# One operation for the home expert's number, own routing for the last list but one, and a new order of work, in a fused attention and mixture-of-experts kernel

## The chip, the cores and the metric

The kernel runs on one core of a Trainium2 chip. The metric is the device time of one execution in microseconds (us), as the median of several runs. Shorter is better.

## The reference

Four batches of 12288 query rows (128 channels) attend to a pooled key map, and each result row is then sent through one of eight experts. What matters of it:

```python
kv_pool = kv.reshape(B, H // r, r, W // r, r, C).mean(axis=(2, 4))
k = v = kv_pool.reshape(B, -1, C) @ w_sr          # 768 keys a batch
s = scale * (q @ k.transpose(0, 2, 1))
a = softmax(s)
x = (a @ v).reshape(-1, C)                        # 49152 rows
logits = x @ w_gate                               # 8 experts
e = argmax(logits, axis=1)
out = softmax(logits)[e] * (relu(x @ w1[e]) @ w2[e])
```

## The kernel before, in words

The rows are worked on in 96 tiles of 512, 24 to a batch. For each tile the attention comes first: four groups of 128 queries, each with its scores on TensorE (PE), the maximum on VectorE (DVE, `maxima`), the exponentials on ScalarE (ACT, `exps`) and a block transpose on DVE (`turn_p`). The turned probabilities go out to memory (`send_p`, in two halves) and come back in another layout (`fetch_p`, two halves), on SP's DMA queue. ACT rounds them to their high half (`high_p`, three pieces), GpSimd (POOL) makes the low half (`low_p`), and PE multiplies both with the values (`values`). Nearly every product is made of three matmuls like this, out of high and low halves (`mm3`, lines 424 to 427), so each operand has a `high` and a `low` step; `high` and `low` themselves are lines 409 and 412. Tiles 0 and 1 go another way: their probabilities are turned on PE (`turn_first`, line 709).

Then comes the routing, by units of one or two tiles (tiles 0 and 1 of a batch are units of their own, the rest are pairs; 52 units). It makes the logits, the one-hot choice of expert and the gate. Each batch has one home expert, the one that the most rows of its first tile choose. `home` (line 904) counts votes on PE and makes, on DVE, `av`, its maximum `top`, the mask `pick` (line 917), the product `pks` of the mask with the expert numbers (line 920), and its sum, the number of the home expert (line 924). That number is read by SP, which loads this expert's weights. All rows of a batch go through the home expert (`experts`: eight blocks of `first`, `high_h`, `low_h` and `second`, then the output). Rows that chose another expert, the strays, are written into lists in memory: `ranks` and `lists` make their places on PE and DVE, `places` on POOL, `order_x` on DVE, and `put` (line 974) scatters one small row for each token, four indirect DMAs for a tile, on POOL. A few stray lists are then read back and done at the end (`ending`), and their rows are scattered over the output (line 1326).

A unit's lists are written when the next unit is routed, so the last unit but one is written with the routing of tile 95, and the last unit behind it, its scatters at a late due time (`put_last`).

The order of work on every engine and queue is written out by hand. Each step has a due time in units of which a tile has 16: a base time from the table `AT` (and from the tile's number), to which the table `MOVE` adds a correction for one named step. A heap (`Plan.run`) takes the steps by due time and issues their instructions, and every engine then runs its own in that order:

```python
key = (*of, fn.__name__, *(x for x in args if not isinstance(x, (float, dict))))
plan.at(t + MOVE.get(key, 0.0), fn, *args)
```

Until tile 0's experts begin the scores have two pairs of PSUM banks; after it they have one, and three banks serve the experts' hidden blocks (lines 391, 1385 to 1394).

Of the kernel before, what the change touches and what calls it, by code (L numbers as in the profile page):

```python
# [21 lines left out]
P = 128  # L22
# [22 lines left out]
    'lists_after': 6.0, 'put_after': 1.5, 'put_last': 66.0, 'turn_y': 2.13, 'move_y': 0.65, 'fetch_y': 6.15,  # L45
# [34 lines left out]
    ('all', 'ask'): 0.0608, ('all', 'fill_pads'): -4.1416, ('all', 'go', 2): -0.6912, ('all', 'go', 3): -5.5634,  # L80
    ('keys', 0, 'pool_head', 4, 0, 4): -0.398, ('keys', 0, 'pool_head', 4, 2, 1): 0.0428, ('keys', 1, 'low_kv', 0):
    0.5914, ('keys', 1, 'pool', 0, 2): -3.677, ('keys', 1, 'pool', 5, 3): 0.1037, ('keys', 1, 'rows', 0, 1): 9.8605,
    ('moe', 0, 'first', 1): -1.0383, ('moe', 0, 'first', 3): -0.706, ('moe', 0, 'first', 5): -1.1562, ('moe', 0,
    'first', 7): -0.6168, ('moe', 0, 'low_h', 6): 0.9976, ('moe', 0, 'second', 0): -0.8796, ('moe', 0, 'second', 2):
    -0.9594, ('moe', 1, 'low_h', 1): 0.785, ('moe', 1, 'low_h', 3): 0.7933, ('moe', 1, 'low_h', 7): 0.7654, ('moe',
    16, 'fetch_y'): 0.2111, ('moe', 2, 'low_h', 2): 0.8672, ('moe', 2, 'low_h', 4): 0.8488, ('moe', 21, 'high_h',
    6): 1.0052, ('moe', 21, 'high_h', 7): 1.7775, ('moe', 21, 'second', 4): 0.5351, ('moe', 22, 'high_h', 0): 0.369,
    ('moe', 22, 'high_h', 1): 0.423, ('moe', 22, 'low_h', 7): -0.241, ('moe', 22, 'second', 1): 1.006, ('moe', 23,
    'low_h', 1): -0.607, ('moe', 3, 'low_h', 1): 0.8385, ('moe', 3, 'low_h', 3): 1.2639, ('moe', 3, 'low_h', 5):
    1.0453, ('moe', 3, 'low_h', 7): 1.1582, ('moe', 4, 'low_h', 0): 0.9424, ('moe', 40, 'order_y'): -0.5162, ('moe',  # L90
    41, 'low_h', 4): 0.0097, ('moe', 44, 'fetch_y'): 0.3182, ('moe', 44, 'move_y'): -0.0224, ('moe', 44, 'order_y'):
    -0.1192, ('moe', 45, 'first', 0): 0.1827, ('moe', 45, 'first', 1): -0.5133, ('moe', 45, 'first', 6): -0.6373,
    ('moe', 45, 'high_h', 0): 0.5733, ('moe', 45, 'high_h', 1): 0.2381, ('moe', 45, 'high_h', 2): -0.1508, ('moe',
    45, 'high_h', 4): 0.3703, ('moe', 45, 'high_h', 5): 0.3419, ('moe', 45, 'second', 0): 0.0096, ('moe', 45,
    'second', 1): -0.6265, ('moe', 45, 'second', 4): 0.9203, ('moe', 46, 'fetch_y'): -5.214, ('moe', 46, 'high_h',
    1): 0.4473, ('moe', 46, 'low_h', 2): 0.1479, ('moe', 46, 'order_y'): 0.2087, ('moe', 46, 'store_y'): 0.9537,
    ('moe', 47, 'fetch_y'): -0.0101, ('moe', 47, 'first', 5): -0.82, ('moe', 47, 'high_h', 3): 1.2641, ('moe', 47,
    'high_h', 6): 1.1188, ('moe', 47, 'low_h', 3): 0.0473, ('moe', 47, 'low_h', 6): 0.7816, ('moe', 47, 'low_h', 7):
    0.1061, ('moe', 47, 'second', 0): -0.0776, ('moe', 47, 'second', 1): 0.0425, ('moe', 47, 'second', 4): 0.0501,
    ('moe', 47, 'second', 6): 0.0208, ('moe', 48, 'first', 5): -0.5455, ('moe', 48, 'first', 6): -2.5799, ('moe',  # L100
    48, 'first', 7): -6.5649, ('moe', 48, 'high_h', 1): 0.1424, ('moe', 48, 'low_h', 2): -0.0333, ('moe', 48,
    'low_h', 4): -0.4459, ('moe', 48, 'second', 0): -0.1822, ('moe', 48, 'second', 3): -1.6033, ('moe', 64,
    'fetch_y'): 0.274, ('moe', 64, 'move_y'): 0.6093, ('moe', 68, 'low_h', 7): -0.076, ('moe', 68, 'order_y'):
    -5.5601, ('moe', 69, 'copy_y'): -0.3826, ('moe', 69, 'fetch_y'): -2.4744, ('moe', 69, 'high_h', 4): 0.0321,
    ('moe', 69, 'high_h', 5): 0.0878, ('moe', 69, 'high_h', 6): -0.0689, ('moe', 69, 'high_h', 7): 0.0837, ('moe',
    69, 'low_h', 2): -0.0943, ('moe', 69, 'low_h', 6): -0.2325, ('moe', 69, 'second', 2): 0.6919, ('moe', 69,
    'second', 4): 0.0109, ('moe', 69, 'store_y'): -0.4167, ('moe', 70, 'fetch_y'): -0.0171, ('moe', 70, 'first', 0):
    -1.5594, ('moe', 70, 'first', 1): -0.0868, ('moe', 70, 'first', 5): -0.1211, ('moe', 70, 'high_h', 1): 1.4475,
    ('moe', 70, 'high_h', 4): 0.8979, ('moe', 70, 'high_h', 5): -0.3782, ('moe', 70, 'low_h', 1): -0.0695, ('moe',
    70, 'low_h', 3): 2.9785, ('moe', 70, 'low_h', 5): -0.0731, ('moe', 70, 'move_y'): -0.1231, ('moe', 71, 'first',  # L110
    0): -0.1207, ('moe', 71, 'first', 1): 0.0174, ('moe', 71, 'first', 4): -0.1249, ('moe', 71, 'first', 5): 0.3023,
    ('moe', 71, 'first', 6): -0.4535, ('moe', 71, 'high_h', 4): 0.0746, ('moe', 71, 'high_h', 5): 0.0835, ('moe',
    71, 'high_h', 6): -0.0512, ('moe', 71, 'low_h', 0): -0.0323, ('moe', 71, 'low_h', 1): 0.5487, ('moe', 71,
    'low_h', 2): -0.0736, ('moe', 71, 'low_h', 4): 0.5119, ('moe', 71, 'second', 2): 0.1089, ('moe', 71, 'second',
    6): -0.5769, ('moe', 72, 'first', 0): 0.2274, ('moe', 72, 'first', 5): -0.5999, ('moe', 72, 'high_h', 0):
    0.0123, ('moe', 72, 'high_h', 7): 0.1144, ('moe', 72, 'second', 0): 0.3824, ('moe', 90, 'low_h', 3): 0.6174,
    ('moe', 91, 'high_h', 7): 0.5069, ('moe', 91, 'second', 7): 0.1429, ('moe', 92, 'first', 0): -0.7256, ('moe',
    92, 'high_h', 0): 0.039, ('moe', 92, 'high_h', 1): 0.262, ('moe', 92, 'high_h', 7): 1.5258, ('moe', 92,
    'order_y'): -2.2243, ('moe', 92, 'store_y'): 3.9584, ('moe', 93, 'copy_y'): -0.2268, ('moe', 93, 'fetch_y'):
    -1.0243, ('moe', 93, 'first', 5): -0.7666, ('moe', 93, 'high_h', 5): 0.2107, ('moe', 93, 'low_h', 1): 0.1114,  # L120
    ('moe', 93, 'low_h', 5): -0.2504, ('moe', 93, 'order_y'): -0.0152, ('moe', 93, 'second', 7): -1.7719, ('moe',
    94, 'low_h', 1): 1.2426, ('moe', 94, 'low_h', 6): 1.0005, ('moe', 95, 'second', 1): -0.8013, ('moe', 95,
    'second', 2): -0.8019, ('route', 0, 'gate', 2): 3.3863, ('route', 0, 'go', 0): 1.5515, ('route', 0, 'norm'):
    2.1006, ('route', 1, 'gate', 0): 0.1309, ('route', 1, 'go', 21): -0.2161, ('route', 1, 'go', 22): -0.5587,
    ('route', 1, 'go', 23): 2.8345, ('route', 1, 'keep_x'): 9.1447, ('route', 1, 'onehot'): -0.1545, ('route', 1,
# [100 lines left out]
def tile_pooled_attention_top1_moe(ctx: ExitStack, tc, q, kv, w_sr, w_gate, w1, w2, out):  # L226
# [578 lines left out]
    def route(t, i, own):  # L805
# [98 lines left out]
        def home():  # L904
# [18 lines left out]
            with nc.allow_low_precision("small whole numbers are exact"):  # L923
                nc.vector.reduce_sum(out=num, in_=pks, axis=AX.X)
# [517 lines left out]
```

## Time and profile before

| | |
|---|---|
| median of 3 runs | 1992.07 us (1991.38 to 1992.39) |
| the profiled execution | 1995.03 us |
| its span, first to last instruction | 1993.3 us |
| mean granted clock of TensorE | 0.995 |
| PE, DVE, ACT, POOL busy | 98%, 83%, 70%, 74% of the span |
| DMA queue of SP (q1) | 77.2% of 16 engines |

How to read it: PE is busy nearly all the time, so its idle time is the place to look. The rows below come from views of that one execution. In a row of a timeline the number in square brackets is the time that the engine stood idle before the instruction, and behind it what ended the wait. In a table of stretches each engine has its busy time in the stretch and, in brackets, its number of instructions; then come the granted clock of TensorE as a share of 2.4 GHz, the share of the 16 DMA engines, and what they moved.

### The profile page before, as it was taken

The page shows a single profiled execution, that of the slowest core. Times are in us where ns is not written, and L with a number is a line of the kernel's source. Part 1 is how long each engine was busy: PE and PEld are TensorE (multiplying, and loading weights), DVE is VectorE, ACT ScalarE, POOL GpSimd, SP SyncE. Part 2 cuts the span into 40 slices and gives each one's busy share as a digit, 9 for nine tenths or more (in the row PEclk, how much of TensorE's full clock was granted, in tenths as well). Part 3 has the DMA queues.
Part 4 walks back from the last instruction along what each step waited for, and adds up shares of the span by engine and source line. Part 5 has one row for each costly group of instructions (what it writes and reads, how often), then busy time and mean ns, then how long its engine had stood idle before and what let it go on. Part 6 is the DMA issues. An engine that isn't in the chain of part 4 may idle for free. (4 is left out here: it accounts for less than half of the span.)

```text
span 1993.3 us, 31428 instructions
## 1 busy us (share of the span) xinstructions
PE 1953.7 (98%) x9482; PEld 1643.1 (82%) x9482; DVE 1645.6 (83%) x3066; ACT 1386.3 (70%) x2718; POOL 1484.0 (74%) x1567
## 2 busy tenths in 40 slices
PE   7899999999999999999999999999999999999997
PEld 6788888888788888888878888888887888888885
DVE  5888888988878888888888889888878788888764
ACT  4677676777676767676767767777777676767663
POOL 0567777777786787778787678777778677778884
PEclk9999999999999999999999999999999999999998
DMA  5899999998687788887678878788777777777662
GB/s 160 213 255 256 241 253 238 246 236 236 205 254 244 231 260 237 249 246 243 209 234 244 255 235 243 232 255 256 228 210 241 228 227 221 229 217 234 213 206 62
DMA packets 504085, 457.57 MB, mean 230 GB/s; under 512 B 240208, under 2 KB 443985, under 8 KB 503520
## 3 DMA queue, kind: packets, MB, share of 16 engines
q1 hardware_dynamic: 491296, 455.06, 77.2%
q0 software_dynamic: 12608, 0.40, 0.5%
q8 instruction: 77, 1.26, 0.3%
q14 instruction: 104, 0.85, 0.1%
HBM read 230.76 MB, written 225.25 MB: 229 GB/s over the span
## 5 line engine op out<-in xcount | busy, mean ns | idle before, releaser
L412 POOL TENSOR_TENSOR pt<-pt,pth 128x1024 fp32r<-128x1024 f32 x282 | 675.8, 2412 | 201.8 <-ACT pth L409 176.6
L1221 ACT ACTIVATE hh<-ps 128x512 fp32r<-128x512 f32 x772 | 464.7, 602 | 502.4 <-PE ps L427 487.9
L1227 DVE SCALAR_TENSOR_TENSOR hlow<-ps,hh 128x512 fp32r<-128x512 f32 x768 | 517.9, 682 | 66.7 <-ACT hh L1221 65.9
L644 DVE TENSOR_REDUCE nmax<-ps 128x1 f32<-128x768 f32 x384 | 366.0, 953 | 147.2 <-PE ps L427 143.1
L976 POOL DMA_INDIRECT xs<-row,dst x384 | 381.1, 993 | 135.4 <-issue 85.8
L667 DVE STREAM_TRANSPOSE pb<-prob 128x768 f32<-128x768 f32 x376 | 364.5, 969 | 42.7 <-ACT prob L652 39.5
L652 ACT ACTIVATE prob<-ps,nmax 128x768 f32<-128x768 f32 x384 | 345.0, 898 | 45.1 <-DVE nmax L644 40.6
L426 PE MATMUL ps<-hlow,wt 128*128 128x512 f32 x768 | 302.8, 394 | 6.9 <-DVE hlow L1227 6.9
L425 PE MATMUL ps<-hh,wt 128*128 128x512 f32 x768 | 304.8, 397 | 0.0
L427 PE MATMUL ps<-xh,wt 128*128 128x512 f32 x768 | 302.6, 394 | 1.6 <-POOL wt L412 1.6
L427 PE MATMUL ps<-hh,wt 128*128 128x512 f32 x768 | 302.3, 394 | 0.0
L426 PE MATMUL ps<-xl,wt 128*128 128x512 f32 x768 | 302.0, 393 | 0.0
L425 PE MATMUL ps<-xh,wt 128*128 128x512 f32 x768 | 300.4, 391 | 0.0
L409 ACT CAST pth<-pt 128x1024 fp32r<-128x1024 f32 x282 | 287.2, 1054 | 3.6 <-DMA pt<-pd 3.6
L425 PE MATMUL ps<-kh,qh 128*128 128x384 f32 x768 | 264.0, 344 | 3.3 <-ACT prob L652 3.3
L427 PE MATMUL ps<-kh,ql 128*128 128x384 f32 x768 | 261.3, 340 | 0.0
L426 PE MATMUL ps<-kl,qh 128*128 128x384 f32 x768 | 259.6, 338 | 0.1
L426 PE MATMUL ps<-pt,vh 128*128 128x512 f32 x564 | 222.6, 395 | 1.5 <-POOL pt L412 1.3
L427 PE MATMUL ps<-pth,vl 128*128 128x512 f32 x564 | 222.0, 394 | 0.0
L425 PE MATMUL ps<-pth,vh 128*128 128x512 f32 x564 | 220.4, 391 | 0.0
L964 POOL TENSOR_TENSOR xl<-xt,xh 128x512 fp32r<-128x512 f32 x96 | 152.7, 1591 | 49.4 <-ACT xh L958 43.4
L425 PEld LDWEIGHTS ps<-hh,wt 128*128 128x128 f32 x768 | 144.7, 188 | 49.0 <-issue 18.6
(173 smaller groups left out, 2988.9 us busy)
## 6 DMA issues: line engine op xcount, KB each, us to landing
pd<-pb SPq DMA_DIRECT2D x188, 768.0 KB
pt<-pd SPq DMA_DIRECT2D x144, 768.0 KB
pt<-pd SPq DMA_DIRECT2D x176, 192.0 KB
xd<-xq SPq DMA_DIRECT2D x96, 256.0 KB
yd<-yt SPq DMA_DIRECT2D x95, 256.0 KB
yr<-yd SPq DMA_DIRECT2D x95, 256.0 KB
out_dram<-yo SPq DMA_DIRECT2D x95, 256.0 KB
qb<-in_q_dram SPq DMA_DIRECT2D x376, 64.0 KB
```

The costliest lines, as they stand in the source:

```text
L409: nc.scalar.copy(out=dst, in_=src)
L412: eng.tensor_tensor(out=dst, in0=src, in1=h.bitcast(F32), op=ALU.subtract)
L425: nc.tensor.matmul(out=ps, lhsT=wh, rhs=xh, start=start, stop=False)
L426: nc.tensor.matmul(out=ps, lhsT=wh, rhs=xl, start=False, stop=False)
L427: nc.tensor.matmul(out=ps, lhsT=wl, rhs=xh, start=False, stop=stop)
L644: nc.vector.tensor_reduce(out=nmax, in_=own["s", g][:, :, :NH], op=ALU.max, axis=AX.XY, negate=True)
L652: nc.scalar.activation(out=prob.rearrange("p (h k) -> p h k", h=2), in_=own["s", g][:, :, :NH], func=AF.Exp, bias=own["nmax", g], scale=1. ...
L667: nc.vector.transpose(out=own["pb"][:, g // HG, :, :, :, g % HG], in_=prob)
L964: nc.gpsimd.tensor_tensor(out=placed(own["xl"], "c (q g r) -> c g r q"), in0=placed(own["xt"], "c (g r q) -> c g r q"), in1=placed(own["xh ...
L976: put = nc.gpsimd.indirect_dma_start(out=xs, out_offset=bass.IndirectOffsetOnAxis(ap=unit["dst"][:, g : g + 1].bitcast(U32), axis=0), in_= ...
L1221: nc.scalar.activation(out=hh, in_=own["hp", f], func=AF.Relu)
L1227: nc.vector.scalar_tensor_tensor(out=hl, in0=own["hp", f], scalar=0.0, in1=own["hh", f].bitcast(F32), op0=ALU.max, op1=ALU.subtract,)
```

## The change

Three things are done. In `home` the product `pks` is made straight from `av`, in PSUM, by one operation that compares with the maximum (a pointer to `top`, in SBUF) and multiplies with the expert numbers `eidx` (in SBUF); `pick` is still made, for the lists, but behind the number. The last unit but one is written with its own routing, at tile 93, and the last unit's scatters have the due time of its own routing in place of `put_last`. And `MOVE` has 471 entries where it had 339: 132 are new, 17 have another value, none is gone.

```diff
@@ AT
-    'lists_after': 6.0, 'put_after': 1.5, 'put_last': 66.0, 'turn_y': 2.13, 'move_y': 0.65, 'fetch_y': 6.15,
+    'lists_after': 6.0, 'put_after': 1.5, 'turn_y': 2.13, 'move_y': 0.65, 'fetch_y': 6.15,
@@ home
-            pick = state["pick", b] = rp.tile([P, E], F32, name="pick_home")
-            nc.vector.tensor_scalar(out=pick, in0=av, scalar1=top, scalar2=None, op0=ALU.is_equal)
-            yield
             pks = rp.tile([P, E], F32, name="pks", bufs=1)
-            nc.vector.tensor_tensor(out=pks, in0=eidx, in1=pick, op=ALU.mult)
+            nc.vector.scalar_tensor_tensor(
+                out=pks, in0=av, scalar=top, in1=eidx, op0=ALU.is_equal, op1=ALU.mult
+            )
             yield
             num = state["num", b] = rp.tile([P, 1], I32, name="home_num")
             with nc.allow_low_precision("small whole numbers are exact"):
                 nc.vector.reduce_sum(out=num, in_=pks, axis=AX.X)
+            yield
+            pick = state["pick", b] = rp.tile([P, E], F32, name="pick_home")
+            nc.vector.tensor_scalar(out=pick, in0=av, scalar1=top, scalar2=None, op0=ALU.is_equal)
@@ route
-        for x, w in ((units[k - 1], t + 0.02),) * (k > 0) + ((unit, u + when("ranks", i)),) * (k + 1 == len(units)):
+        late = k + 2 >= len(units)
+        for x, w in ((units[k - 1], t + 0.02),) * (0 < k < len(units) - 1) + ((unit, u + when("ranks", i)),) * late:
...
                 v = u + when("put_x", i) + after * AT["put_after"] + (16 if len(unit["tiles"]) > 1 else 8) * n
-                if k + 1 == len(units):
-                    v = 16 * NS + AT["put_last"] + 8 * n if x is unit else v - 12 * n
+                if x is unit:
+                    v -= 8 * n
                 at(v, put, x, n)
```

Of the entries of `MOVE` these bear on the text below (in plan units, 0 where there was none):

| step | before | after |
|---|---|---|
| tile 2, `high_p 0` | 0 | 2.17 |
| tile 3, `exps 3` | 0 | 0.43 |
| tile 3, `scores 1` | 0 | 0.33 |
| experts of tile 0, `first 5` | -1.16 | -8.31 |
| experts of tile 1, `first 2` | 0 | -11.50 |
| routing of tile 1: `firsts`, `first`, `onehot` | 0, 0, -0.15 | 2.24, 1.84, 1.47 |
| routing of tile 1: `square_x`, `keep_x` | 0.01, 9.14 | 19.02, 17.08 |
| tile 0, `scores 3`; tile 1, `scores 0` | 0, 0 | -3.48, -5.01 |
| tiles 4, 5, 6, `fetch_p 0` | 0, 0, 0 | 4.80, 6.40, 4.01 |
| tile 4, `fetch_p 1` | 0 | 1.95 |
| tiles 8, 11, `load` | 0, 0 | 13.22, 8.79 |
| `load_small` | 0 | 0.11 |
| tile 94, `values 0`, `high_p 1` | 0, 0 | 6.58, -2.20 |
| experts of tile 90, `order_y` | 0 | -5.98 |

Of the 149, 114 lie in the keys of batch 0, the tiles 0 to 11 and their routing and experts, and 24 in the last six tiles and behind them; the others are single steps at the tiles 21 to 25, 46 to 49, 69 to 72.

## Rows read from the trace of the kernel before

**Rows 1.** Table of stretches, the sums: 0 to 220, 200 to 1950, 1850 to 1994 us.
```profile
sum 220.00, PE 203.74 PEld 172.22 DVE 174.65 ACT 140.25 POOL 122.21; mean PE 9.26 PEld 7.83 DVE 7.94 ACT 6.38 POOL 5.55
...
sum 1750.00, PE 1741.11 PEld 1464.39 DVE 1471.52 ACT 1246.27 POOL 1357.51; mean PE 49.75 PEld 41.84 DVE 42.04 ACT 35.61 POOL 38.79
...
sum 144.00, PE 128.81 PEld 106.21 DVE 88.83 ACT 83.12 POOL 100.53; mean PE 8.59 PEld 7.08 DVE 5.92 ACT 5.54 POOL 6.70
```

**Rows 2.** PE's waits over the whole run: us in total, times, longest.
```profile
PE ps L464 <- DVE pt L472: 7.3, 2, 7.0
PE ps L426 <- DVE hlow L1227: 6.9, 8, 1.9
...
PE ps L709 <- ACT prob L652: 2.2, 5, 0.6
PE ps L427 <- POOL wt L412: 1.6, 2, 1.1
```

**Rows 3.** Timeline of DVE, the four products of home: start us, us, instruction.
```profile
52.26 0.79 DVE L920 TENSOR_TENSOR pks<-eidx,pick_home 128x8 f32<-128x8 f32 x1
...
535.03 5.45 DVE L920 TENSOR_TENSOR pks<-eidx,pick_home 128x8 f32<-128x8 f32 x1
...
1018.75 3.28 DVE L920 TENSOR_TENSOR pks<-eidx,pick_home 128x8 f32<-128x8 f32 x1
...
1500.85 3.71 DVE L920 TENSOR_TENSOR pks<-eidx,pick_home 128x8 f32<-128x8 f32 x1
```

**Rows 4.** Timeline of POOL beside the second of them.
```profile
535.68 4.77 POOL L412 TENSOR_TENSOR pt<-pt,pth 128x1024 fp32r<-128x1024 f32 x2
```

**Rows 5.** Timeline of PE at tiles 24 and 72: matmuls that waited.
```profile
541.33 0.50 PE L426 MATMUL ps<-hlow,wt 128*128 128x512 f32 x1 [1.57 <-DVE hlow L1227]
...
545.08 0.50 PE L426 MATMUL ps<-hlow,wt 128*128 128x512 f32 x1 [1.42 <-DVE hlow L1227]
...
1506.12 0.50 PE L426 MATMUL ps<-hlow,wt 128*128 128x512 f32 x1 [1.86 <-DVE hlow L1227]
```

**Rows 6.** Table of stretches, two with a lower clock.
```profile
80.00:90.00 10.00, 10.00 (x41) 8.44 (x40) 6.86 (x10) 5.32 (x11) 6.57 (x6) 0.83 0.99 232
...
1505.00:1510.00 5.00, 3.88 (x11) 2.91 (x12) 4.51 (x13) 1.33 (x3) 2.14 (x11) 0.69 0.72 213
```

**Rows 7.** View of single lines of home: duration in ns, least, median, most.
```profile
L909 DVE SCALAR_TENSOR_TENSOR ps<-ps,wdesc x4: 162/165/174, 51.6 to 1500.2; 128x8 f32<-128x8 f32 x4
...
L917 DVE TENSOR_SCALAR pick_home<-ps,top x4: 215/226/226, 52.0 to 1500.6; 128x8 f32<-128x8 f32 x4
```

**Rows 8.** Timelines of PE and ACT, 60 to 80 us, and the page's `pth` group.
```profile
65.75 0.44 PE L425 MATMUL ps<-kh,qh 128*128 128x384 f32 x1 [1.32 <-ACT prob L652]
...
78.95 0.44 PE L425 MATMUL ps<-kh,qh 128*128 128x384 f32 x1 [1.77 <-ACT prob L652]
...
76.48 1.05 ACT L409 CAST pth<-pt 128x1024 fp32r<-128x1024 f32 x1 [3.07 <-DMA pt<-pd]
...
L409 ACT CAST pth<-pt 128x1024 fp32r<-128x1024 f32 x282 | 287.2, 1054 | 3.6 <-DMA pt<-pd 3.6
```

**Rows 9.** The end: POOL's last scatter, and SP's wait.
```profile
1981.17 0.97 POOL L976 DMA_INDIRECT xs<-row,dst  x1 [0.30 <-DMA xs<-row,dst]
...
SPq L1438 <- DMA xs<-row,dst: 3.6, 1, 3.6
```

**Rows 10.** Timelines of POOL and PE in the last 75 us.
```profile
1923.77 1.87 POOL L950 TENSOR_TENSOR pos<-pos,oh 128x8 f32<-128x8 f32 x7 [0.49 <-DVE pos L938]
...
1931.53 2.43 POOL L412 TENSOR_TENSOR pt<-pt,pth 128x1024 fp32r<-128x1024 f32 x1
...
1965.28 0.48 PE L425 MATMUL ps<-xh,wt 128*128 128x512 f32 x1
```

**Rows 11.** Timelines of DVE and POOL at 1800 us: a pointer in SBUF.
```profile
1804.01 0.73 DVE L1147 TENSOR_SCALAR idx<-cell,lift 128x4 int32<-128x4 f32 x1
...
1799.94 4.77 POOL L412 TENSOR_TENSOR pt<-pt,pth 128x1024 fp32r<-128x1024 f32 x2 [0.32 <-ACT pth L409]
```

More of the change, by code (lines that the diff above doesn't have):

```diff
@@ L79 @@
 MOVE = {
[L80 to L84, printed above, removed]
@@ L90 @@
[L90 to L94, printed above, removed]
@@ L95 @@
[L95 to L109, printed above, removed]
@@ L185 @@
-    ('weights', 3, 'rest', 1): 7.0254, ('weights', 3, 'where'): 0.0374,
+    ('all', 'ask'): 0.0608, ('all', 'count'): -0.2523, ('all', 'fill_pads'): -4.1416, ('all', 'go', 0): -0.2522,
+    ('all', 'go', 2): -0.6912, ('all', 'go', 3): -5.5634, ('all', 'load_small'): 0.105, ('all', 'spare'): -1.8341,
+    ('keys', 0, 'high_kv', 4): 0.5384, ('keys', 0, 'low_kv', 3): 0.0678, ('keys', 0, 'mean', 1): -0.378, ('keys', 0,
+    'mean', 3): 0.0904, ('keys', 0, 'pool_head', 1, 0, 4): -1.5167, ('keys', 0, 'pool_head', 4, 0, 4): -0.398,
@@ new lines @@
+    ('route', 0, 'high_x'): -1.716, ('route', 0, 'norm'): 2.1006, ('route', 1, 'first'): 1.8386, ('route', 1,
+    'firsts'): 2.2373, ('route', 1, 'gate', 0): -0.2415, ('route', 1, 'gate', 1): 1.0313, ('route', 1, 'gate', 2):
+    18.3197, ('route', 1, 'go', 20): -15.7246, ('route', 1, 'go', 21): -0.2161, ('route', 1, 'go', 22): -0.5587,
+    ('route', 1, 'go', 23): 2.9978, ('route', 1, 'high_x'): 0.8148, ('route', 1, 'keep_x'): 17.0778, ('route', 1,
+    'logits'): 0.0152, ('route', 1, 'onehot'): 1.4682, ('route', 1, 'order_x'): -0.0134, ('route', 1, 'put', 0):
@@ new lines @@
+    'keep_x'): -2.3788, ('route', 71, 'below'): -0.1401, ('route', 71, 'firsts'): 0.2312, ('route', 71, 'gate', 0):
+    0.1882, ('route', 71, 'go', 20): -17.613, ('route', 71, 'go', 21): -4.175, ('route', 71, 'go', 23): 0.8656,
+    ('route', 71, 'high_x'): -1.2576, ('route', 71, 'low_x'): 0.1691, ('route', 71, 'put', 1): -11.5949, ('route',
+    71, 'totals'): 0.5289, ('route', 71, 'turn_logits'): -0.2782, ('route', 72, 'firsts'): 0.0702, ('route', 72,
+    'gate', 0): -0.2439, ('route', 72, 'gate_exp'): 0.0418, ('route', 72, 'go', 0): 1.5845, ('route', 72, 'go', 5):
@@ new lines @@
+    -0.1399, ('route', 72, 'keep_x'): -8.3825, ('route', 72, 'logits'): 0.2125, ('route', 72, 'low_x'): 0.3338,
+    ('route', 72, 'norm'): -0.143, ('route', 72, 'put', 0): 1.389, ('route', 72, 'put', 1): 11.4169, ('route', 73,
+    'put', 0): 12.9634, ('route', 93, 'below'): 0.1621, ('route', 93, 'high_x'): -0.1634, ('route', 93, 'keep_x'):
+    -1.2067, ('route', 93, 'norm_logits'): -0.2316, ('route', 93, 'ranks'): -0.1351, ('route', 93, 'turn_logits'):
+    -0.6197, ('route', 94, 'norm'): 1.0227, ('route', 95, 'below'): -0.1515, ('route', 95, 'firsts'): -0.0084,
@@ L186 @@
+    ('tile', 95, 'values', 1): -7.7438, ('weights', 0, 'cut', 1): 0.7711, ('weights', 0, 'rest', 1): 1.1867,
+    ('weights', 2, 'rest', 1): 0.1356, ('weights', 3, 'cut', 1): 0.0778, ('weights', 3, 'rest', 1): 7.0254,
+    ('weights', 3, 'where'): 0.0374,
 }
```

203 lines of the change are left out of this document (124 added, 79 removed).

## The prediction

> **What bounds the kernel now.** I read the table of stretches first, for where TensorE (PE) is idle [rows 1]. From 80 us to 1960 us PE is busy almost all of the time: 16.3 us of its idle time lie in the first 220 us (220.00 less 203.74), all of it before 80, 8.9 us in the whole middle (1750.00 less 1741.11) and 15.2 us at the end (144.00 less 128.81). So a stall of PE taken away comes off the end, and engines other than PE cost only where PE waits for them. The list of PE's waits gives their names [rows 2]: 7.3 us for the first keys (nearly all of it one wait, before which there is no data), 6.9 us for the low half of a hidden block made by VectorE (DVE), 2.2 us for exponentials, 1.6 us for a split weight. The timelines around the longest of these say why, and each part below takes its own.
>
> **The home number (four times, tiles 0, 24, 48, 72).** In the timeline of DVE the product `pks<-eidx,pick_home`, 128x8, takes 5.45, 3.28, 3.71 and 0.79 us [rows 3], where the sum `av`, of its size, takes at most 0.174 [rows 7]. It started at 535.03 and ended at 540.48; the GpSimd (POOL) pair of subtractions beside it ran from 535.68 to 540.45 [rows 4]. The product has both operands in SBUF and ends when POOL stops. Behind it in DVE's queue stand the subtractions that make the low halves, and PE waits for these 1.57 and 1.42 us at tile 24 and 1.86 us at tile 72 [rows 5]. Of the other 2.05 us of [rows 2]'s 6.9, in five shorter waits, I take 1.4 for tile 48, whose product took 3.28. That is 4.85 + 1.4 = 6.3 us. After the wait at 1506 the granted clock fell to 0.69 in a 5 us window [rows 6], half speed, 1.2 GHz, for part of it: 5 x 0.31 = 1.6 us. Gain of this part: 7.9 us.
>
> The row shows a wait that goes past the end of the first of POOL's two instructions (4.77 us for both). The Trainium skill (SBUF — State Buffer, Who interferes with whom) says that a VectorE instruction with two SBUF inputs contends with a GpSimd one that reads SBUF, and that the second to issue blocks until the first finishes. By that rule the product would have been let through at the first boundary, the 3.0 us at tile 24 would not hang on it, and the sum below would be 12.3 us (1979.8) in place of 15.3. I go by the row.
>
> The change makes the product straight from `av` in PSUM with the maximum as a pointer, and puts `pick` behind the number. No row shows that form (PSUM, SBUF pointer, SBUF tensor). The nearest are `av` itself, PSUM with an SBUF tensor, 162 to 174 ns in all four, and `pick`, PSUM with an SBUF pointer, 215 to 226 ns [rows 7]; at tile 24 both ran while POOL was at work. So I take 0.2 us and no wait; the other end is the wait of now, a gain of nothing. One instruction less on DVE, 4 x 0.2 us, is off the path.
>
> **The first 80 us.** The new order follows from due time plus `MOVE`. The longest stall there, 1.77 us at 78.95, is for the exponentials of tile 3, group 3; ScalarE (ACT) stood 3.07 us before them, at the copy `pth` of tile 2 that waits for a DMA [rows 8]. Its due time is 32 + 28.75 = 60.75, the exponentials' 61.78. The change moves them to 62.92 and 62.21: the exponentials go first, and 1.77 us goes. What is late next is `pth` itself, which waits for the same DMA. The clock at half speed behind it (0.83 in 80 to 90 us, [rows 6]) is 10 x 0.17 = 1.7 us. The stall of 1.32 us at 65.75 [rows 8] is for tile 3, group 0: its maximum stood behind tile 1's one-hot chain. `firsts`, `first` and `onehot` move 1.5 to 2.2 behind it, three small DVE operations, and `moe 0 first 5` (three matmuls at a pitch of some 0.23 us, 0.7) goes ahead of the waiting scores (due 52.29 against 52.33). I take 0.9. The split weight is waited for 1.1 us at most [rows 2]; the number comes 0.8 us sooner (0.79 to 0.2, `pick` off its path), but PE comes sooner too: 0.5. Transposes of tiles 0 and 1 wait 2.2 us for exponentials [rows 2]; the next scores now go ahead of the transpose in four places, and exponentials ahead of copies on ACT: half, 1.1. Together 1.77 + 1.7 + 0.9 + 0.5 + 1.1 = 6.0. Lower end: a new wait eats all, 0 (a loss is the third rival). Upper end: all of the 16.3 but the 7.0 us before the first data [rows 2], and the clock: 9.3 + 1.7 = 11.0.
>
> On SP's queue the loads of tiles 8 and 11 go 13.2 and 8.8 later, `fetch_p 0` of tiles 4 to 6 goes 4.0 to 6.4 later, behind `send_p 1`, `keep_x` of tile 1 behind a fetch, and `load_small` behind the second block of keys. All high halves of a tile wait for both fetches, and the second moves by 1.9 at one tile alone, so I cost these at nothing; what hides them is that after the 3.07 us only 0.5 us of the run's `pth` waits are for a DMA (3.6 in all, [rows 8]). If that cover goes, it is the third rival.
>
> **The end.** Now the last unit's eight scatters are due at 1602 and 1610, and those of the unit before at 1577.5 and 1581.5. New: 1586.5 and 1594.5, and 1554.5 and 1562.5. POOL's last scatter ran to 1982.14, and SP waited 3.6 us for its landing before it could close the kernel [rows 9]. With eight scatters (some 10 us) gone from POOL's last stretch the stores of the last tile's rows end the kernel. When they land is not shown: between no gain and the whole 3.6 I take 2.0, about the middle, as stores and scatters are issued in the same microseconds.
>
> What this costs: `places` of unit 50 now stands ahead of tile 95's first low half on POOL, 1.87 us for seven sums, and 2.2 with the product behind them, an estimate; POOL had a 0.49 us wait before the same step of unit 49 [rows 10], which an earlier position on DVE removes. The low half ran at 1931.53 with PE close behind. Between nothing and 2.2 us I take 0.6. Tile 95's `low_x` falls behind eight more scatters, 10 us at 0.97 and a gap of 0.3 each. From 1931.53 on POOL has three low halves of 2.4, a `low_x` of half their elements and twelve scatters, at most 25 us, and is at tile 95's `low_x` by 1957; PE reaches that tile's experts at 1965.28 [rows 10]. The eight microseconds hide it; without them PE would wait for what is over.
>
> At tiles 21 to 25, 46 to 48, 69, 72 a dozen steps change places with a neighbour; each moves one operation of 0.7 us past another. No cost.
>
> **Sum.** 7.9 + 6.0 + 2.0 - 0.6 = 15.3 us. The profiled execution took 1995.03 us with a span of 1993.3; it lies 3.0 us above the median of 1992.07. Nothing shows that 3.0 us of difference to lie in a stall named here, so I set the sum against the median: 1992.07 - 15.3 = **1976.8 us**. A measurement of this kernel can tell about 0.2%, 4.0 us, from no change.
>
> **The rivals.** *The product still waits for POOL.* The change then doesn't do what its first part says. For it: `idx<-cell,lift`, one SBUF tensor and an SBUF pointer, took 0.73 us and ended at 1804.74, with POOL's 4.77 us at 1804.71 [rows 11]; a pointer and a tensor in SBUF may be enough. Against: [rows 7]. Then 7.9 is lost: 1984.7. Chance 0.11. The Trainium skill (VectorE: DVE Perf Modes, Why PSUM operands drop a tier) has another reason for that row: a single-source instruction may use both SBUF read ports for one tensor, which a PSUM operand rules out; by that the new form is free.
>
> *The start gives nothing*, because one reordered step waits for something new, as PSUM banks held longer by `moe 0 first 5`: 1992.07 - 9.3 = 1982.8. For it: seven matmul groups move at once where three banks serve. Against: each of them goes ahead of work that only waits now. Chance 0.11. With the rival above as well: 1990.7, no change, chance 0.03.
>
> *Slower: late fetches.* In 80 to 90 us the DMA share is 0.99 [rows 6]. If `fetch_p` of tiles 3 to 6, put back by up to 8 us (6.4 plan units; 24 tiles of 16 units take 484 us from 535.03 to 1018.75, [rows 3]), lands so late that PE waits 6 us at each of four tiles, 24 us come back: 1992.07 - 15.3 + 24 = 2000.8. It decides from 4.8 us a tile on (15.3 + 4.0 over four). Against: the second fetch, which must be waited for anyway, hardly moves. Chance 0.02.
>
> **How the numbers follow.** Forecast 0.73, rivals 0.11, 0.11, 0.03 and 0.02. Faster by over 0.2%: 0.73 + 0.11 + 0.11 = 0.95; same 0.03; slower 0.02. The range takes in both single rivals, up to 1985.5. Downward the start may give 3.5 more, the end 1.6 and the 0.6 may not be paid: 1976.8 - 5.7 = 1971.1, put at 1971.5.
>
> **What would show it.** `pks` at 0.2 us four times, and no wait of PE for `hlow` over 0.5 us at tiles 24, 48, 72; the granted clock at 1.00 there; no ACT wait for a DMA before the exponentials at 75 to 79 us; PE idle under 11 us in the first 80; POOL done before PE at the end. Wrong would be: `pks` over 1 us beside POOL, a new PE wait for `pt` between 90 and 160 us, or one of 2 us near 1934.

## The result and the profile after

The changed kernel takes **1970.42 us** (median of 4 runs, 1969.98 to 1971.55) against 1992.23 for the kernel before beside it: 21.8 us less, a ratio of 0.9891 [0.9874, 0.9908]. The forecast of 1976.8 had the right sign and most of the size; the result lies 1.1 us below the lower end of its range.

The profiled execution took 1969.98 us with a span of 1968.3, at a mean granted clock of 0.999. First the sums of the table of stretches (0 to 220, 200 to 1950, 1850 to 1970 us), which answer to [rows 1]:

```profile
sum 220.00, PE 208.16 PEld 176.22 DVE 178.03 ACT 144.74 POOL 127.53; mean PE 34.69 PEld 29.37 DVE 29.67 ACT 24.12 POOL 21.25
...
sum 1750.00, PE 1747.45 PEld 1471.35 DVE 1463.84 ACT 1250.53 POOL 1368.04; mean PE 873.72 PEld 735.67 DVE 731.92 ACT 625.26 POOL 684.02
...
sum 120.00, PE 111.19 PEld 91.15 DVE 74.58 ACT 69.91 POOL 84.07; mean PE 55.59 PEld 45.57 DVE 37.29 ACT 34.95 POOL 42.04
```

PE is idle for 11.8 us of the first 220 (16.3 before) and for 2.6 of the middle 1750 (8.9 before). PE's waits say which are gone; they answer to [rows 2] (us in total, times, longest):

```profile
PE ps L505 <- DVE pt L513: 8.1, 2, 7.0
...
PE ps L467 <- POOL pt L453: 1.7, 2, 1.0
...
PE ps L750 <- ACT prob L693: 1.2, 3, 0.6
PE ps L468 <- POOL wt L453: 1.0, 1, 1.0
...
PE ps L467 <- DVE hlow L1271: 0.5, 2, 0.3
```

The 6.9 us for `hlow` are now 0.5, the exponentials' 2.2 are 1.2, and the two waits for POOL's `pt` are 1.7 in all, the longer one, of 1.0, new (before they were 1.3, at most 0.7). For [rows 3]: the view of the number's line (least, median, most in ns, and when).

```profile
L958 DVE SCALAR_TENSOR_TENSOR pks<-ps,top,eidx x4: 216/226/228, 50.5 to 1486.5; 128x8 f32<-128x8 f32 x4
```

Timelines of DVE and POOL at tile 24, which answer to [rows 3, 4]:

```profile
527.93 0.23 DVE L958 SCALAR_TENSOR_TENSOR pks<-ps,top,eidx 128x8 f32<-128x8 f32 x1
...
527.67 4.80 POOL L453 TENSOR_TENSOR pt<-pt,pth 128x1024 fp32r<-128x1024 f32 x2
```

And the page's group of `pth`, for [rows 8]:

```profile
L450 ACT CAST pth<-pt 128x1024 fp32r<-128x1024 f32 x282 | 287.0, 1053 | 0.0
```

The product started 0.26 us behind POOL's pair and was done in 0.23 us, in its midst. The granted clock is 1.00 in the 5 us behind tile 72's number, where [rows 6] has 0.69. ACT no longer waits for a DMA before any `pth`.

**Where the gain comes from.** PE does the same work in both kernels, so I line up the starts of one matmul, the gate product of each unit: there are 52 in a run, and how much earlier each starts in the changed kernel is the gain collected so far. One such row of before and its partner after (tile 95's):

```profile
1947.67 0.62 PE L831 MATMUL ps<-xt,wgate 128*8 128x256 f32 x8
```

```profile
1931.28 0.62 PE L872 MATMUL ps<-xt,wgate 128*8 128x256 f32 x8
```

That is 16.39 us of the 25.0 by which the spans of these two profiles differ (1993.3 and 1968.3). As the profile of before lay 3.0 us above the median, the terms are read from a second pair, copies of both kernels run side by side (d_before and d_after below, spans 1989.9 and 1969.2):

| gate product | d_before | d_after | earlier by | gained since the row above |
|---|---|---|---|---|
| 5th mark (behind the start) | 187.45 | 184.05 | 3.40 | 3.40 start |
| 14th (ahead of tile 24's number) | 526.40 | 522.96 | 3.44 | 0.04 |
| 15th (behind it) | 550.28 | 542.79 | 7.49 | 4.05 home |
| 27th | 1009.87 | 1002.27 | 7.60 | 0.11 |
| 28th (behind tile 48's) | 1032.70 | 1022.41 | 10.29 | 2.69 home |
| 40th | 1491.77 | 1481.46 | 10.31 | 0.02 |
| 41st (behind tile 72's) | 1516.37 | 1502.40 | 13.97 | 3.66 home |
| 51st | 1913.77 | 1899.79 | 13.98 | 0.01 |
| 52nd (tile 95) | 1945.26 | 1932.59 | 12.67 | -1.31 cost of the lists |
| PE's last matmul | 1977.44 | 1963.94 | 13.50 | 0.83 |
| end of the span | 1989.9 | 1969.2 | 20.7 | 7.2 close of the kernel |

So **home gives 10.4** (4.05 + 2.69 + 3.66), **the start 3.4**, **the close 7.2**, and the lists cost 1.3, of which 0.8 comes back in the last stretch. That is 20.7 us; the 1.1 us between it and the 21.8 of the result lie between sets of runs and belong to no term.

**The close.** The prediction held that SP's wait for the last scatter [rows 9] closes the kernel. More rows of the kernel before show what else stood there. SP's waits (total, times, longest):

```profile
SPq L1438 <- PEq L1438: 6.3, 2, 5.8
```

The view of its last line (three drains of a queue: least, median, longest in ns; first start and last end):

```profile
L1438 POOLq DRAIN  x3: 45/107/6278, 1986.2 to 1993.0; - x3
L1438 SPq DRAIN  x3: 7/7/13, 1986.8 to 1992.7; - x3
```

SP's waits in the changed kernel:

```profile
SPq L1482 <- SPq L1482: 3.1, 1, 3.1
...
SPq L1482 <- DMA out_dram<-yr: 1.3, 1, 1.3
...
SPq L1482 <- PEq L1482: 0.7, 2, 0.5
```

The view of its last line, and the end of POOL's timeline:

```profile
L1482 POOLq DRAIN  x3: 45/107/6278, 1959.3 to 1968.0; - x3
```

```profile
1955.27 0.97 POOL L1370 DMA_INDIRECT out_dram<-yo,tok  x1 [0.30 <-ACT hh L1265]
```

POOL closes with a drain of 6.28 us. Before, POOL's last instruction ended at 1982.14 [rows 9], behind PE (1979.86); the drain began 4 us later, at 1986.2, and the span ended at 1993.3, 13.44 us behind PE's last matmul. What fills those 4 us stands in the view of the line ahead of it (least, median, longest in ns; first and last start):

```profile
L1406 POOLq EVENT_SEMAPHORE  x4: 17/43/3532, 1977.7 to 1980.9; - x4
L1406 POOLq INC_SWDGE_SEM  x1: 1715/1715/1715, 1984.4 to 1984.4; - x1
```

So the landing of the last scatter is the first link of the close and not the last: POOL's queue waits for it from 1980.9 to 1984.4 (in d_before the trace has the landing at 1980.99 and the end of the same wait at 1981.02), spends 1.72 us on one more instruction, and only then begins the drain. SP's 3.6 us of [rows 9] end at 1986.3, behind that instruction and not with the landing. SP began its own drains at 1986.8 and then waited 5.8 us; the list puts that down to PE's queue, but PE had long been done, and what ran until then was POOL's drain. In all five profiles in which POOL is done that late (before, d_before, e1, e3, e5) the span ends 0.83 to 0.84 us behind the end of that drain. Now POOL is done at 1956.24, 6.4 us ahead of PE (1962.65): the drain, from 1959.3 to about 1965.6, lies beside PE's last work and SP's last stores, and the span ends 5.6 us behind PE.

### The profile page after: what moved, and what is told of

Its sections match the earlier page's. It is cut to its first block, busy times and chain, and to the rows that moved or that the text cites. A ratio compares the mean times of both kernels' runs of the same rounds, so it can differ in the third digit from the quotient of the medians.

```text
span 1968.3 us, 31430 instructions
## 1 busy us (share of the span) xinstructions
PE 1947.8 (99%) x9482; PEld 1639.7 (83%) x9482; DVE 1632.8 (83%) x3066; ACT 1387.4 (70%) x2718; POOL 1483.6 (75%) x1567
## 4 chain that ended last, share of the span: by engine, by line
PE 94%; DVE 2%; POOL 1%; ACT 1%; issue 1%; DMA 1%; SPq 0%; DVEq 0%; POOLq 0%; ACTq 0%
PE ps L466 30%; PE ps L467 30%; PE ps L468 30%; PE ps L872 1%; POOL pt L453 1%; PE ps L505 1%; DMA pb<-in_kv_dram 0%; ACT prob L693 0%; DVE nmax L685 0%; PE ps L561 0%; POOL xs L1019 0%; PE ps L562 0%; DVE pb L708 0%; DVE hlow L1271 0%; POOL ql L453 0%
```

## The experiments

Times are medians, and each ratio is against the kernel before, run in the same set on the same chip. There are four sets: e1 to e4, then c and e5, e6, then d and s, then f and g. One thing has to be said of the first two sets: there PE's last stretch, from tile 95's gate product to PE's end, took 35 to 44 us in every kernel profiled, in place of the 31 to 32 of the others, which moves the times of those sets by some microseconds. It isn't the chip alone: the second and the third set ran on the same one. The units of home take as long in every set, but for those at tiles 48 and 72 in c_after and e5, which are 1.0 to 1.5 us longer than in d_after.

**The number alone (e1_home).** The kernel before with the new product, `pick` behind the number, and nothing else.

```diff
-            nc.vector.tensor_tensor(out=pks, in0=eidx, in1=pick, op=ALU.mult)
+            nc.vector.scalar_tensor_tensor(
+                out=pks, in0=av, scalar=top, in1=eidx, op0=ALU.is_equal, op1=ALU.mult
+            )
```

> The kernel before with the new home alone (product by one operation out of PSUM, pick behind the number); order of work and lists as before. Theory 1 (the product's wait for POOL is the whole of the home term, and it is larger than I forecast because the stall is followed by smaller ones): matched starts of PE's gate product give 4.1 us between tiles 23 and 25, 2.8 between 47 and 49 and 3.6 between 71 and 73, so 10.5 us less than before in all three, and the start, the end and their idle times are as before: some 1981.7 for a before of 1992.2. Theory 2 (part of the 10.5 comes from the moved steps of the middle; the product gives what the forecast said): 7.9 us less, 1984.3. In both pks takes 0.2 to 0.25 us four times.

Measured: 1985.89, ratio 0.9966 [0.9952, 0.9979], 6.5 us less. In the trace all four products take 0.22 to 0.23 us, and against d_before the three units of tiles 24, 48 and 72 are shorter by 3.14, 2.27 and 3.43 us, 8.8 in all, between the two theories' 7.9 and 10.5. The edit works alone, for some nine microseconds of PE's time up to tile 95. The profiled execution, 1983.1, shows all of it (9.3 under the median of before); the other four runs took 1985.7 to 1986.1, and what they lose isn't known, as none of them has a trace.

**The moved steps of the start alone (e3_start).** The kernel before with the 111 other due times of the first keys and tiles 0 to 11, among them:

```diff
+    ('tile', 2, 'high_p', 0): 2.1747, ('tile', 3, 'exps', 3): 0.427,
-    ('moe', 0, 'first', 5): -1.1562,
+    ('moe', 0, 'first', 5): -8.3142,
```

> The kernel before with the moved steps of the start alone (keys of batch 0, tiles 0 to 11 with routing and experts, weights of batch 0); home and end as before. Theory 1 (the start's term stands by itself): the gate product of tile 4 starts 6 to 7.2 us earlier than before, and the difference stays until tile 23: some 1985.6 for 1992.2. Theory 2 (the start's gain hangs on the new home, whose number frees the first split weight 0.8 us sooner, and without it the new order meets new waits): 5 us or less, 1987.5 or more.

Measured: 1987.90, 0.9976 [0.9966, 0.9987], 4.5 us less. Its fifth mark is at 183.78, where copies of the kernel before have 186.82 and 187.45 and the first profile 189.93. That is the second theory's size (1987.5 or more), but the new order met no new wait without the new home: with it the stretch from the first mark to the fifth is as long (137.7 us in both).

**The new lists and the moved steps at the end alone (e2_end, and g_end once more).**

```diff
-        for x, w in ((units[k - 1], t + 0.02),) * (k > 0) + ((unit, u + when("ranks", i)),) * (k + 1 == len(units)):
+        late = k + 2 >= len(units)
+        for x, w in ((units[k - 1], t + 0.02),) * (0 < k < len(units) - 1) + ((unit, u + when("ranks", i)),) * late:
...
-                if k + 1 == len(units):
-                    v = 16 * NS + AT["put_last"] + 8 * n if x is unit else v - 12 * n
+                if x is unit:
+                    v -= 8 * n
```

> The kernel before with the end alone: the last list but one with its own routing, the last unit's scatters at the due time of its own routing, and the moved steps from tile 88 on. Theory 1 (before, the kernel's end hangs on POOL: behind its last scatter it has some 4 us and a drain of 6.28 us, and the others wait for that): PE's last operation comes at about the same time as before (within 1 us), but the time from there to the end of the span falls from 13.4 to about 5.7 us: 7 to 8 us less in all, some 1985. Theory 2 (the forecast: only the landing of the scatters goes): 2.0 less 0.6 = 1.4 us less, some 1990.8, and the drain still closes the span.

> The kernel before with the end alone, again, in a call with a control of its own. In its first call it took 3.5 us more than before, with a last stretch of 39.7 us. Theory 1 (that stretch was a disturbance of the call, which before hides under POOL's close and this kernel doesn't): if the control's stretch is 31.4 us here, this one's is too, the time behind PE's last operation is 5.6 us, and it takes some 6.5 us less than before, 1985.4 for 1991.9; if the control's is 35 us or more, it takes as much as before or more. Theory 2 (the new end by itself makes the long stretch): 39 us again, whatever the control has.

Measured: e2_end 1995.84, 1.0016 [1.0007, 1.0025]; g_end, the same program, 1986.52, 0.9975 [0.9966, 0.9984]. PE's last stretch took 39.69 us in the one and 31.33 in the other, and both end 5.2 to 5.6 us behind PE. The first answer, taken by itself, would have made this part of the change a loss; it gives 5.0 us where the last stretch isn't stretched (6.5 was expected).

**The old number in the new order (e4_oldhome).** The changed kernel with `pick` first and the product of two SBUF operands again.

```diff
-            nc.vector.scalar_tensor_tensor(
-                out=pks, in0=av, scalar=top, in1=eidx, op0=ALU.is_equal, op1=ALU.mult
-            )
+            nc.vector.tensor_tensor(out=pks, in0=eidx, in1=pick, op=ALU.mult)
```

> The kernel after with the old home (pick first, product of two SBUF tensors behind it); all else as after. Theory 1 (home's term is the product's wait alone, whatever the order around it): the three stretches of PE at tiles 24, 48 and 72 take 10.5 us longer again: some 1981 for an after of 1970.4. Theory 2 (the moved steps of the middle now put other work between the product and the low halves PE needs): 5 us or less of it comes back, 1975 or less.

Measured: 1987.80, 0.9975 [0.9966, 0.9984]. The view of the line (ns), and POOL's timeline at tile 24:

```profile
L961 DVE TENSOR_TENSOR pks<-eidx,pick_home x4: 167/2856/4139, 50.6 to 1492.5; 128x8 f32<-128x8 f32 x4
```

```profile
527.64 4.72 POOL L453 TENSOR_TENSOR pt<-pt,pth 128x1024 fp32r<-128x1024 f32 x2
```

The wait is back. The three units of home take 23.00, 22.69 and 24.54 us; against d_after's 19.83, 20.14 and 20.94 that is 9.3 us. Of the 10.4, then, the moved steps at these tiles give 1.1 (1.6 if e1's 8.8 is taken) and the new product the rest.

**PSUM or the number of operations? (e6_avsbuf)** The changed kernel, with the one operation, but `av` in SBUF.

```diff
-            av = table("av", E, 1)
+            av = rp.tile([P, E], F32, name="av", bufs=1)
```

> The kernel after with av in SBUF in place of PSUM; the new operation for the product then has both tensors and the pointer in SBUF. Theory 1 (what lets the product pass POOL is that one tensor comes out of PSUM): pks takes 3 to 5.5 us again at the tiles 24, 48 and 72 where POOL is at work, PE waits there, and the time is some 10 us longer. Theory 2 (what counts is that the product is made in one operation, or where it now stands in the order): pks stays at 0.2 to 0.3 us, and the time is as after.

Measured: 1991.03, 0.9971 [0.9959, 0.9983], against 1982.63 for the copy of the changed kernel in the same set. The same two views:

```profile
L958 DVE SCALAR_TENSOR_TENSOR pks<-av,top,eidx x4: 228/3094/4555, 52.3 to 1495.6; 128x8 f32<-128x8 f32 x4
```

```profile
529.59 4.74 POOL L453 TENSOR_TENSOR pt<-pt,pth 128x1024 fp32r<-128x1024 f32 x2
```

The same instruction, with the same pointer in SBUF, takes up to 4.56 us when its first operand lies in SBUF, and the gain at the three tiles is gone (23.14, 23.06 and 24.59 us; 7.4 us more than c_after's units). What counts is the operand in PSUM, not the operation saved: with it there, a pointer in SBUF and one tensor in SBUF beside it do not make DVE wait. Without a PSUM operand they may: the `idx<-cell,lift` of [rows 11] ends 0.03 to 0.04 us behind a subtraction of POOL, after 0.73 to 0.74 us, in the first profile, the changed kernel's and both d copies, where its second instance takes 0.19.

**Does POOL's last instruction end the kernel? (e5_poolend, beside copies c_after and c_before)** The changed kernel with a copy of 128x1 on POOL behind the last tile's rows.

```diff
+            own["mark"] = rp.tile([P, 1], F32, name="mark", bufs=1)
+            nc.gpsimd.tensor_copy(out=own["mark"], in_=own["yo_1"][:, G - 1, :1])
```

> The kernel after, unchanged. The kernel with the old home in it (all else as after) took 1987.8, which is 17.4 more than the 1970.4 of after; its trace has 10.5 less of that at the three home tiles, as expected, and some 8 us at the end: from the gate product of tile 95 to PE's last operation it needs 38.9 us where after needed 30.9, with every engine's order the same. Theory 1 (the 8 us are the old home's, or chance in how it was laid out): after takes 1970.4 again, 30.9 us in its last stretch. Theory 2 (the 8 us depend on the chip or on the run, and after's profile happened to miss them): after takes some 1978 here, 38 to 39 us in its last stretch.

> The kernel before, unchanged, for a second profile of it: its first one lay 3.0 us above the median of its runs. Theory 1 (the 3.0 us lie in the end, which differs from run to run): up to the gate product of tile 95 the two profiles agree within 0.5 us, and PE's last stretch (31.75 us in the first profile) or the time behind it (13.4 us) is shorter here where the run is near 1992.2. Theory 2 (they lie in the start or at the home tiles): the difference shows there.

> The kernel after with one more instruction at the very end of POOL: it copies one number for each partition out of the last output rows, so it starts when DVE has made them, some 1.3 us after PE's last operation and 7 us after POOL's last scatter. Theory 1 (POOL's end costs a fixed time behind its last instruction, whatever it is: 3 to 4 us and then the drain of 6.28 us and 0.8): the span ends some 11 us behind the copy, 5 to 6 us later than after. Theory 2 (the drain waits for scatters in flight and is over when they have landed): no difference, within 1 us.

Measured: c_after 1982.63, 0.9926 [0.9912, 0.9939]; c_before 1996.13 (one run); e5_poolend 1986.36, 0.9949 [0.9935, 0.9962], which is 3.7 more than c_after. The end of POOL's timeline, the last line and SP's waits in e5_poolend:

```profile
1975.21 0.19 POOL L1366 COPY mark<-yr 128x1 f32<-128x1 f32 x1 [7.21 <-DVE yr L1357]
```

```profile
L1484 POOLq DRAIN  x3: 45/107/6280, 1977.3 to 1984.1; - x3
```

```profile
SPq L1484 <- PEq L1484: 5.3, 2, 4.8
```

A copy of 0.19 us, late on POOL, brings back the whole close: the drain of 6.28 us, SP's long wait, a span that ends 9.0 us behind the copy and 9.9 behind PE (5.6 in c_after). The cost is below the 5 to 6 us of the first theory, for behind a copy there is no landing to wait for: the drain begins 1.9 us behind it, against 3.0 to 4.1 behind the scatters that end POOL's work in the kernels with all of them. The drain asks for no scatter in flight; it comes behind whatever POOL does last, a scatter or a copy. Its length is not one for all programs, as the next experiment shows.

**The scatters themselves (s1_after_noscat, s2_before_noscat, d_after, d_before; g_noscat, g_after).** Both kernels without the 16 scatters of the last two units, and copies of both. The rows of `xs` that these scatters write are left out.

```diff
-            for g in range(n * G, (n + 1) * G):
+            for g in range(n * G, (n + 1) * G if unit["k"] < len(units) - 2 else 0):
```

> The kernel after without the sixteen scatters of the last two units (their rows are left out of the lists, all other work is done). Theory 1 (scatters one behind the other hold up what the other engines tell each other): the last stretch takes 31 to 32 us on every chip, so this is faster than after by what after's stretch is above 31.4 us: 0 to 10 us by the chip. Theory 2 (the stalls belong to the chip or to the other work of the end): the last stretch is as long as after's in this call, within 1 us. By both the time behind PE's last operation stays at 5.6 us.

> The kernel before without the sixteen scatters of the last two units (rows left out of the lists, as in the second kernel). POOL's last instruction is then the second scatter into the output, before PE's end. Theory 1 (POOL's close costs before some 8 us behind PE, and the scatters cost the rest of the stretch): the last stretch falls to 31 to 32 us and the time behind PE's last operation from 13.4 (or 9.8) to 5.5 us; some 8 us less than before on a chip without the stalls. Theory 2 (forecast): at most 3.6 us less.

> The kernel after, unchanged, as the control of this call's chip. So far its last stretch (gate product of tile 95 to PE's last operation) took 31.4 us on one chip and 41.4 on another, with the same order of work and with engines that stand idle together, beside POOL's row of scatters. Theory 1 (the stalls come with the scatters that run one behind the other there): some 1970 to 1983, as the chip has it, with the surplus over 31.4 us in the stretch where POOL scatters. Theory 2 (the stalls have nothing to do with the scatters): the same time; the next kernel tells the two apart.

> The kernel before, unchanged, as the control of this call's chip. Theory 1 (POOL closes the kernel): the span ends 11.2 us behind POOL's last scatter, whatever PE's last stretch takes, unless that takes so long (44 us in the second profile) that the stores end it, 5.3 us behind PE's last operation. Theory 2 (as forecast, only the landing of the scatters closes it): the end follows the landing, less than 4 us behind POOL's last scatter.

> The kernel after without the sixteen scatters of the last two units (their rows are left out), again. In an undisturbed call it took what after takes. Theory 1 (in a disturbed call the scatters make the stalls): where the control has 35 us or more in its last stretch, this one has 31 to 32. Theory 2 (they have no part in it): as long as the control's. In an undisturbed call the two don't part.

> The kernel after, unchanged, the control of the call. 31.4 us in its last stretch and some 1970.7 in an undisturbed call, 35 to 42 us and 1974 to 1983 in a disturbed one.

Measured: d_before 1991.70 and s2_before_noscat 1984.45, 0.9960 [0.9946, 0.9974]; d_after 1970.90, 0.9889 [0.9873, 0.9906], and s1_after_noscat 1970.88, 0.9893 [0.9876, 0.9909]; g_after 1970.84, 0.9897 [0.9881, 0.9912], and g_noscat 1971.54, 0.9900 [0.9885, 0.9916]. In the kernel before, leaving out the 16 scatters is worth 7.3 us; in the changed one, nothing. The drain is shorter without them, 4.97 us, in all three kernels that leave them out. SP's waits and the last line in s2_before_noscat:

```profile
SPq L1438 <- DMA out_dram<-yr: 1.2, 1, 1.2
...
SPq L1438 <- PEq L1438: 0.7, 2, 0.5
```

```profile
L1438 POOLq DRAIN  x3: 45/107/4972, 1971.4 to 1981.8; - x3
```

PE ends at 1976.48 in it and at 1977.44 in d_before, but the span ends 5.6 behind PE in place of 12.5. So 6.9 of the 7.9 us between these two profiles lie in the close: SP's wait of 5.8 us is gone, as in the changed kernel. That the last stretch of PE is 31.35 us with and 31.36 without the scatters (d_after and s1) shows that in the changed kernel they cost PE nothing.

**Can the cost be taken back? (f1_lowfirst)** The changed kernel with tile 95's first low half ahead of `places` of unit 50 on POOL, and one low half of tile 90 half a unit earlier.

```diff
-            at(u + when("places", i) + after, places, x)
+            at(u + when("places", i) + after + (2.5 if after and k + 2 == len(units) else 0), places, x)
...
+    ('tile', 90, 'low_p', 0): -0.5,
```

> The kernel after with two steps of POOL turned round: tile 95's first low half goes ahead of the places of unit 50 (2.5 units later), and tile 90's ahead of the second gather of a list (0.5 units earlier). Theory 1 (the waits of 0.98 us near 1918 and 0.73 us near 1803 come from what stands ahead of these low halves on POOL, and nothing else is late behind them): both waits are gone, and PE reaches the gate product of tile 95 1.5 to 1.9 us earlier than after against the same start; the time falls by as much, 1969 for 1970.7, which is less than the runs can tell. Theory 2 (places or the gather are late next): other waits of 0.5 us or more stand in their place and less than 1 us is gained.

Measured: 1970.94, 0.9897 [0.9882, 0.9912], the same as g_after beside it (1970.84). First the timelines of PE and POOL in the changed kernel, PE's new wait and POOL ahead of it:

```profile
1917.64 0.50 PE L467 MATMUL ps<-pt,vh 128*128 128x512 f32 x1 [0.98 <-POOL pt L453]
...
1912.92 1.91 POOL L993 TENSOR_TENSOR pos<-pos,oh 128x8 f32<-128x8 f32 x7
...
1915.19 2.40 POOL L453 TENSOR_TENSOR pt<-pt,pth 128x1024 fp32r<-128x1024 f32 x1
```

Then those of f1_lowfirst, the same step of POOL and what PE and DVE wait for later:

```profile
1913.92 2.41 POOL L453 TENSOR_TENSOR pt<-pt,pth 128x1024 fp32r<-128x1024 f32 x1 [0.41 <-DVE ps L987]
...
1946.98 1.13 PE L1259 MATMUL ps<-xt,pb 128*128 128x128 f32 x8 [1.05 <-DVE qt L1303]
...
1944.04 0.22 DVE L1015 TENSOR_REDUCE dst<-pos 128x8 int32<-128x64 f32 x1 [0.98 <-POOL pos L994]
```

The 0.98 us went, as the swap should make it, and came back 30 us later: `places` is later, DVE waits 0.98 for its sums, and PE 1.05 behind DVE. The last stretch grew from 31.36 (g_after) to 32.42. The other swap did less than expected: the wait near 1803 is still there, 0.69 us after 0.72. So this gives nothing back.

## Why the prediction was right, and where it was not

**The failed step is the end term**: "POOL's last scatter ran to 1982.14, and SP waited 3.6 us for its landing before it could close the kernel [rows 9]", from which came "between no gain and the whole 3.6 I take 2.0". The landing was taken for the last thing that the kernel waits for. It is the first: behind it, in POOL's own queue, come 1.72 us of another instruction and the drain of 6.28 us. In the same list of SP's waits stood 5.8 us for another engine's end, and in the view of the last line the drain; both were left out, and so the term's upper bound of 3.6 lay at half of what the close cost. The term measures 7.2 in the pair and 7.3 where the scatters alone are left out; e5 shows the drain as the mechanism. The direction, that POOL would be done before PE, was right (1956.24 and 1962.65), and so was its cause. With 7.2 for 2.0 the sum would have given 1971.6, just inside the range. The range itself was drawn tighter than its parts: it lets the start give 3.5 more, where the start's own upper end (11.0) is 5.0 above the 6.0 taken.

**Home was right in the wait and low in its size**: 7.9, against 8.8 (e1) to 9.3 (e4) for the product and 10.4 with the moved steps. The value of 0.2 us for a form that no row showed held (0.216 to 0.228), and no wait for `hlow` is over 0.3 us. Of the 7.9 only 6.3 were the wait, and that part is too low: the forecast added up the waits behind the product for `hlow`, where the ledger counts the whole unit, and it costed the moved steps at nothing ("a dozen steps change places with a neighbour" gave some 1.1). The other 1.6, for the half clock at tile 72, has nothing behind it. In c_before, e3, g_end and s2 the clock stays at 1.00 all through that unit, and it takes 24.4 to 24.5 us; in the first profile, d_before and e2 it falls, and the unit takes 24.5 to 24.6. PE is idle for longer in it where the clock holds (2.6 to 2.9 us against 1.9). That the two mistakes have opposite signs is luck. The stretch of [rows 6] in c_before (us, busy time of each engine with instructions, then granted clock, DMA share, GB/s):

```profile
1505.00:1510.00 5.00, 4.17 (x20) 3.29 (x20) 3.36 (x8) 3.80 (x7) 2.84 (x8) 1.00 1.03 320
```

On the reason, e6 decides. The form with both tensors in SBUF waits across POOL's instruction boundary again: it started at 529.81 and ended at 534.36, with POOL's pair ending at 534.33. The Trainium skill (SBUF — State Buffer, Who interferes with whom) calls the shared port pair an exclusive lock. Read as held for one POOL instruction (some 2.4 us), it would let the product through at the first boundary; the traces disagree with that in three kernels now (5.45 in [rows 3], 4.14 in e4, 4.56 in e6). The same section of the Trainium skill says that a VectorE instruction with two SBUF inputs contends with a GpSimd one that reads SBUF; e6 against the changed kernel agrees (4.56 against 0.23 us): the operand in PSUM is what makes the wait go.

**The start was sized from one execution and was too high**: 6.0 forecast, 3.4 in the pair, 4.5 by e3's medians. Its two largest terms, the stall of 1.77 us at 78.95 and the 1.7 us of half clock behind it [rows 6], were added up, and of the seven profiles with the old order of the start only the first has both. d_before has the stall (1.84) at full clock. The other five (c_before, e1, e2, g_end, s2) have no such stall, but there the granted clock falls sooner, between 60 and 75 us, about the wait of 1.32 us that all seven have, and 1.7 to 3.4 us go by it. The stretch of [rows 6] in d_before, then the one where the clock falls in c_before:

```profile
80.00:90.00 10.00, 10.00 (x48) 8.56 (x47) 7.99 (x13) 5.23 (x12) 6.09 (x6) 1.00 1.06 243
```

```profile
60.00:70.00 10.00, 7.61 (x29) 6.17 (x28) 8.80 (x24) 6.55 (x13) 7.08 (x8) 0.83 0.82 188
```

and in the changed kernel:

```profile
80.00:90.00 10.00, 10.00 (x48) 8.56 (x47) 8.31 (x14) 7.26 (x13) 4.18 (x6) 1.00 1.05 268
```

From the first mark to the fifth the old order takes 141.0 to 143.3 us in its seven profiles, longest in the first; the new order takes 137.6 to 137.7 in all eleven that have it, with the clock at 1.00 from 50 to 115 us in each. So behind the first mark the new order gives 3.3 to 5.6 us, by what the old one happens to lose. The first mark itself comes at 45.0 to 47.8 us, whatever the order; in the pair it came 0.7 us later in d_after, which is why the 4.1 us gained behind it show as 3.4.

Against the first profile the start did give 7.1 (189.93 to 182.80 at the fifth mark), but that execution is not the usual one: against d_before it is 1.0 us late at the first mark and 2.5 at the fifth, and its close is 1.0 longer. The sentence "Nothing shows that 3.0 us of difference to lie in a stall named here" is where this slipped: about half of it lay in the two terms of the start, which I subtracted from the median as if every run paid both. Home's shortfall and the start's excess cancel (13.9 us forecast and 13.8 measured), which is luck again, so the whole miss shows as the end term's.

**The cost** of the new lists is 1.3 (0.6 forecast, bounds 0 and 2.2), by the mechanism named: POOL's seven sums (1.91) ahead of tile 95's low half, and PE behind it. 0.8 of it returns before PE ends.

The rivals fell as the traces show them: the product doesn't wait for POOL, the start gives something, and no fetch came late (`pth`'s waits are 0.0). Of the list of signs, PE's idle time in the first 80 us came out at 11.8 us where I wrote under 11; 8.1 of it is for the first keys, 7.0 in one wait.

Left open is why the last stretch takes 35 to 44 us in the first two sets. In those traces several engines stand idle together with no releaser that the profile can name; a row of ACT in c_before and one in c_after:

```profile
1981.05 1.57 ACT L1221 ACTIVATE hh<-ps 128x512 fp32r<-128x512 f32 x3 [5.72 <-remote]
```

```profile
1939.23 0.60 ACT L1265 ACTIVATE hh<-ps 128x512 fp32r<-128x512 f32 x1 [4.37 <-issue]
```

The kernel before hides up to some 7 us of that behind POOL's close, the changed one nothing, which is why the gain was 14.5 us in that set and 20.7 to 21.8 elsewhere. Whether the scatters have a part in it could only be tried in sets where the stretch wasn't long, and there they have none.

## What to carry to other kernels

Look at what each engine does behind its last instruction, and have GpSimd done well before the engine that ends last: here the way it closed was worth 7.2 of 20.7 us, though its share of busy time said nothing of it. Follow the chain of waits to the end of the span: the first wait found there need not be the last. A small VectorE operation on the critical path that runs beside GpSimd should read one of its tensors from PSUM. Add up a stall and a clock loss only where more than one execution has both, or set the sum against the execution it was read from.

## What the runs showed of the hardware that was not expected

POOL's close takes a drain of 6.28 us, begun 2 to 4 us behind its last instruction, whether that is a scatter or a copy of one column; it is 4.97 us with 16 scatters fewer in the program. Beside POOL's pair of subtractions, VectorE's 128x8 product takes 0.23 us with one tensor in PSUM and, with both in SBUF, 2.09 to 5.45, until the pair has ended. The old order of work came through its first 110 us with up to 3.1 us of difference between executions, the new one, from the first gate product to the fifth, with less than 0.1. And a fall of the granted clock, though 1.7 us of clock time go by it in tile 72's unit, left that unit at most 0.2 us longer than where the clock held.
